# Top-k attention and a hard-swish feed-forward: weighted values queued behind the scores of a later duo, left-over keys first among the scores

## The chip, the cores and the metric

The kernel runs on one core of one Trainium2 chip. The metric is the device time of one execution in microseconds (us). A core has TensorE (PE in the profile; its weight loads are PEld), VectorE (DVE), ScalarE (ACT), GpSimd (POOL) and SyncE (SP), which here issues the DMAs. Each has its own queue of instructions; semaphores hold an instruction until what it needs is there.

## The reference

```python
# attention: q, k, v are (8 batches, 8 heads, 576 positions, 64)
scores = scale * np.matmul(q, k.transpose(0, 1, 3, 2))
kth = np.partition(scores, -32, axis=-1)[..., -32:-31]
scores = np.where(scores >= kth, scores, -1e9)
attn = np.exp(scores - np.max(scores, axis=-1, keepdims=True))
attn = attn / (np.sum(attn, axis=-1, keepdims=True) + 1e-09)
attn_out = np.matmul(attn, v)
# feed-forward: x is (4608 tokens, 512), w_in (512, 2048), w_out (2048, 512)
x = attn_out.transpose(0, 2, 1, 3).reshape(4608, 512)
h = x @ w_in
out = (h * np.clip(h + 3.0, 0.0, 6.0) / 6.0) @ w_out
```

Every row of scores keeps its 32 largest entries. All is float32; the feed-forward weights arrive in a wider type and are converted at the start.

## The kernel before

**Duos.** Two heads make a pair, two pairs a duo. A duo is one tile of 128 queries for two pairs, four heads in all. The 576 positions are 4 x 128 and 64 left over, so besides the usual duos there are *rest* duos, which hold the 64 left-over queries (`self.rest`). There are 80 duos, ten a batch (`per_batch`), numbered `m`. In batches 3 to 6 the rest duos are the third and the eighth of the ten; in the others two rest duos follow each other.

**The steps of a duo.** `scores` (L200) multiplies queries by keys into one PSUM tile of five banks, `big`. In a usual duo each of the four heads has a contraction of 64 and uses half of the array's rows (L227, eight records in the profile, two halves at a time): *row halves*. The 64 left-over keys of a pair's two heads lie side by side in `kr`, with zeros elsewhere, and take one matmul over the full array (L230). A rest duo uses quarters (L215, L217). ScalarE copies the tile to `sc` (L233, L236). `top` (L243) is VectorE's search: four rounds of MAX8 (L250) and MATCH_REPLACE8 (L254) for each pair. Then for each pair `shift` (POOL, L263, L266), `exp` (ACT, L273, L278, L283), `inverse` (DVE, L287), `weights` (POOL, L297 and the copy L306 to 16-bit halves `e16`), `flip` (a transposing DMA from SP, L312, to `t16`), and `join` (a copy to `eT`, L318, by ACT for the first pair and by POOL for the second). `values` (L326) multiplies the weights by v into `pv`: each head writes half of the columns (L338, 40 records): *column halves*. `place` (ACT, L348) copies `pv` to `xT`, the input of the feed-forward.

**Feed-forward.** `feed_forward` (L352) handles a block of 128 tokens: 64 matmuls to `h` (L365) and 16 to `acc` (L385); the profile has two records for each such float32 matmul. It is a generator that gives its matmuls in 16 *pieces*, each of eight matmuls to h or two to acc. ACT makes `g` and `hs` of h (L373, L375), POOL gates them (L379, L380), ACT scales `acc` to `o` (L395) and SP stores it (L397). 36 blocks make 576 pieces.

**Order.** The schedule is written by hand. For each duo the main loop (L562) runs eight *slots*, i = 0 to 7. A slot issues one round of `top`, then what is due, and then pieces. The scores of duo m+1 are issued at slot i = 1 of duo m. The other steps stand in tables of slots, counted from the first slot of their own duo: `usual` (L532), `early` for the first two duos and `soon` for the last two. How many pieces a slot gets follows from `left`, the number that are queued (L595). At i = 3 of the second and third duo of a batch, `load_values` issues eight DMAs for v from SP (L163, L167). They overwrite `vm` and `vr`, so they wait for the last values of the batch before.

**Buffers.** `kq` and the transposed weights, `e16`, `t16`, `eT` and the landing tiles share the pool `kqpool` (L57), 13 buffers of one size. `big` has one buffer in PSUM; `pv`, `h` and `acc` share three.

Of the kernel before, what the change touches and what calls it, by code (L numbers as in the profile page):

```python
# [29 lines left out]
def kernel(  # L30
# [9 lines left out]
    nc = tc.nc  # L40
# [12 lines left out]
    def pool(name, bufs, **kw):  # L53
        return ctx.enter_context(tc.tile_pool(name=name, bufs=bufs, **kw))

    consts = pool("consts", 1)
    kqpool = pool("kq", 13)  # L57
    scpool = pool("sc", 3)
    wkpool = pool("wk", 1)
    mpool = pool("m", 4)  # L60
# [27 lines left out]
    def big():  # L88

        return ps_big.tile([P, 5 * 512], F32, tag="big", name="big")  # L90
# [94 lines left out]
    class Duo:  # L185
# [14 lines left out]
        def scores(self, us=(0, 1)):  # L200

            if us[0] == 0:
                self.sc = scpool.tile([P, 2, 2 * (S + R)], F32, tag="sc", name="sc")
                self.den = mpool.tile([P, 2, 2], F32, tag="den", name="den")
            sc, nu = self.sc[:, us[0] : us[-1] + 1, :], len(us)
            ps = big()
            heads = [slice(0, D), slice(D, P)]
            qs = slice(self.qt * P, min(self.qt * P + P, S))
            banks = ps[:, 0 : 4 * 512].rearrange("p (n s) -> p n s", s=512)
            left = ps[:, 4 * 512 :]  # L210
            if self.rest:
                for i, u in enumerate(us):
                    pr = self.pairs[u]
                    for d in heads:
                        nc.tensor.matmul(banks[d, i, :], pr.qT[d, qs], pr.kT[d, :])  # L215
                    for hh, d in enumerate(heads):
                        nc.tensor.matmul(left[d, i * R : (i + 1) * R], pr.qT[d, qs], pr.kr[d, hh, :])  # L217
                nc.gpsimd.memset(sc[:, :, S : S + R], 0.0)
                nc.scalar.copy(sc[:, :, 0:JP], banks[:, 0:nu, :])
                nc.scalar.copy(  # L220
                    sc[:, :, JP:S], left[:, 0 : nu * R].rearrange("p (u r) -> p u r", r=R)
                )
                return
            for i, u in enumerate(us):
                pr = self.pairs[u]
                for hh, d in enumerate(heads):
                    nc.tensor.matmul(banks[:, 2 * i + hh, :], pr.qT[d, qs], pr.kT[d, :])  # L227
            for i, u in enumerate(us):
                pr = self.pairs[u]
                nc.tensor.matmul(  # L230
                    left[:, i * P : (i + 1) * P], pr.qT[:, qs], pr.kr[:].rearrange("p h r -> p (h r)")
                )
            nc.scalar.copy(  # L233
                sc.rearrange("p u (h s) -> p (u h) s", h=2)[:, :, 0:JP], banks[:, 0 : 2 * nu, :]
            )
            nc.scalar.copy(  # L236
                sc[:, :, JP : JP + P], left[:, 0 : nu * P].rearrange("p (u r) -> p u r", r=P)
            )
# [177 lines left out]
    per_batch = 2 * J + 2  # L416
    ND = len(duos)
# [92 lines left out]
    def pair_at(m, first):  # L510
# [21 lines left out]
    usual = dict(  # L532
        shift0=3, exp0=4, inverse0=9, weights0=10, flip0=12, join0=15,
        shift1=7, exp1=8, inverse1=13, weights1=14, flip1=16, join1=19, values=22, place=23,
    )
    early = dict(
        shift0=3, exp0=3, inverse0=4, weights0=4, flip0=5, join0=8,
        shift1=7, exp1=7, inverse1=8, weights1=8, flip1=9, join1=12, values=12, place=13,
    )
    soon = dict(  # L540
        shift0=3, exp0=3, inverse0=5, weights0=5, flip0=7, join0=10,
        shift1=7, exp1=7, inverse1=9, weights1=9, flip1=11, join1=14, values=16, place=17,
    )
    queued = {}
    for m in range(ND):
        for part, at in (early if m < 2 else soon if m >= ND - 2 else usual).items():
            queued.setdefault(8 * m + at, []).append((m, part))

    def parts(slot, late=None):
# [12 lines left out]
    for m in range(ND + 3):  # L562
        u = duos[m] if m < ND else None
# [70 lines left out]
```

## Time and profile before

| | |
|---|---|
| median of 4 runs | 1582.98 us (1582.19 to 1584.37) |
| the profiled execution: its own time | 1583.64 us |
| the profiled execution: span of its trace | 1581.9 us |
| VectorE busy | 1466.6 us |
| TensorE busy | 1469.5 us |
| ScalarE busy, GpSimd busy | 1092.6 us, 1141.9 us |
| L250, mean of one MAX8 | 744 to 747 ns |
| L385, L365, L338, L227: busy | 524.9, 543.6, 225.7, 135.8 us |
| granted TensorE clock, mean | 0.963 |

The span runs from the first instruction of the trace to its last. The busy time of TensorE is taken from records whose ends are modelled, so that starts are surer than ends. An entry of the timeline gives the start, the time from the first start to the last end of a merged run of instructions, the engine, line and operation, the tiles (out<-in), and in brackets the idle time of the engine just before it with what ended it.

### The profile page before, as it was taken

The page shows a single profiled execution, that of the slowest core. Times are in us where ns is not written, and L with a number is a line of the kernel's source. Part 1 is how long each engine was busy: PE and PEld are TensorE (multiplying, and loading weights), DVE is VectorE, ACT ScalarE, POOL GpSimd, SP SyncE. Part 2 cuts the span into 40 slices and gives each one's busy share as a digit, 9 for nine tenths or more (in the row PEclk, how much of TensorE's full clock was granted, in tenths as well). Part 3 has the DMA queues.
Part 4 walks back from the last instruction along what each step waited for, and adds up shares of the span by engine and source line. Part 5 has one row for each costly group of instructions (what it writes and reads, how often), then busy time and mean ns, then how long its engine had stood idle before and what let it go on. Part 6 is the DMA issues. An engine that isn't in the chain of part 4 may idle for free.

```text
span 1581.9 us, 28785 instructions
## 1 busy us (share of the span) xinstructions
PE 1469.5 (93%) x10272; PEld 1031.1 (65%) x10272; DVE 1466.6 (93%) x3105; ACT 1092.6 (69%) x1865; POOL 1141.9 (72%) x1264
## 2 busy tenths in 40 slices
PE   5256899799999999999999999999999999999899
PEld 2152666467766776766676776777767776767665
DVE  6999999999999999999999999999999999899800
ACT  6675777677776777677776777778767777777521
POOL 4868687677867787777687777877687777867741
PEclk9577799999999999999999999999999999999999
DMA  8652544444444444455344444445353543533410
GB/s 236 163 177 45 112 83 88 86 91 97 76 99 82 97 83 89 88 97 105 65 101 73 97 88 83 92 93 112 57 110 76 97 88 83 97 63 68 82 23 14
DMA packets 450319, 144.49 MB, mean 91 GB/s; under 512 B 433280, under 2 KB 441472, under 8 KB 450176
## 3 DMA queue, kind: packets, MB, share of 16 engines
q1 hardware_dynamic: 450176, 142.65, 44.2%
q8 instruction: 81, 1.33, 0.4%
q14 instruction: 62, 0.51, 0.1%
HBM read 45.09 MB, written 9.44 MB: 34 GB/s over the span
## 4 chain that ended last, share of the span: by engine, by line
PE 54%; DVE 34%; POOL 4%; issue 3%; ACT 3%; DMA 1%; SPq 1%; POOLq 0%; ACTq 0%; DVEq 0%
PE acc L385 20%; PE h L365 20%; DVE m L250 17%; DVE wk L254 14%; PE pv L338 6%; PE big L227 4%; PE big L230 1%; PE big L177 1%; DVE y L118 1%; PE big L215 1%; POOL eT L318 1%; POOL e L306 1%; DMA t<-e 1%; DVE a L117 1%; POOL sc L297 1%
## 5 line engine op out<-in xcount | busy, mean ns | idle before, releaser
L250 DVE MAX8 m<-wk 128x8 f32<-128x576 f32 x864 | 613.6, 747 | 2.2
L385 PE MATMUL acc<-w_out,g 128*128 128x512 f32 x1152 | 524.9, 604 | 15.3 <-POOL g L380 15.3
L365 PE MATMUL h<-xT,w_in 128*128 128x128 f32 x4096 | 484.1, 278 | 3.0 <-ACT xT L348 3.0
L365 PEld LDWEIGHTS h<-xT,w_in 128*128 128x128 f32 x4096 | 471.6, 194 | 17.3 <-issue 11.9
L254 DVE MATCH_REPLACE8 wk<-m,wk 128x576 f32<-128x576 f32 x576 | 424.0, 743 | 0.0
L385 PEld LDWEIGHTS acc<-w_out,g 128*128 128x128 f32 x1152 | 213.1, 193 | 251.6 <-issue 229.3
L297 POOL TENSOR_SCALAR sc<-sc,den 128x576 f32<-128x576 f32 x288 | 213.3, 751 | 192.0 <-DVE den L287 185.1
L306 POOL COPY e<-sc 128x2304 uint16<-128x2304 uint16 (+1 forms) x192 | 320.0, 1676 | 10.1
L278 ACT ACTIVATE sc<-sc,shift 128x576 f32<-128x576 f32 x288 | 220.4, 771 | 28.4 <-POOL shift L266 25.6
L338 PE MATMUL pv<-eT,vm 128*64 128x128 f32 (+1 forms) x2560 | 164.4, 273 | 67.4 <-ACT eT L318 45.2
L318 ACT COPY eT<-t 128x2304 uint16<-128x2304 uint16 (+1 forms) x82 | 216.1, 2635 | 9.3 <-DMA t<-e 9.3
L273 ACT ACTIVATE sc<-sc,m 128x576 f32<-128x576 f32 x288 | 210.4, 780 | 12.1 <-DVE m L250 11.8
L254 DVE MATCH_REPLACE8 wk<-m,sc 128x576 f32<-128x576 f32 x288 | 212.0, 743 | 0.0
L318 POOL COPY eT<-t 128x2304 uint16<-128x2304 uint16 (+1 forms) x78 | 203.8, 2613 | 9.7 <-DMA t<-e 9.6
L250 DVE MAX8 m<-sc 128x8 f32<-128x576 f32 x288 | 203.5, 744 | 4.2 <-ACT sc L236 4.2
L338 PEld LDWEIGHTS pv<-eT,vm 128*64 128x64 f32 x2560 | 135.1, 141 | 104.5 <-ACT eT L318 46.7
L373 ACT ACTIVATE g<-h,three 128x512 f32<-128x512 f32 x144 | 98.3, 683 | 143.5 <-PE h L365 132.5
L380 POOL TENSOR_TENSOR g<-g,hs 128x512 f32<-128x512 f32 x144 | 184.7, 1282 | 12.1
L379 POOL TENSOR_SCALAR g<-g 128x512 f32<-128x512 f32 x144 | 89.0, 618 | 109.9 <-ACT g L373 101.2
L233 ACT COPY sc<-big 128x2048 f32<-128x2048 f32 (+1 forms) x65 | 119.5, 1838 | 38.7 <-PE big L230 38.1
L227 PE MATMUL big<-kq 64*128 64x512 f32 x512 | 135.8, 651 | 8.6 <-ACT kr L183 5.0
L395 ACT ACTIVATE o<-acc 128x512 f32<-128x512 f32 x36 | 21.4, 593 | 112.8 <-PE acc L385 112.8
(47 smaller groups left out, 1117.0 us busy)
## 6 DMA issues: line engine op xcount, KB each, us to landing
landed<-in_k_dram SPq DMA_DIRECT2D x64, 128.0 KB, 2.9
landed<-in_q_dram SPq DMA_DIRECT2D x64, 128.0 KB, 2.9
st<-in_moe_w_in_dram SPq DMA_DIRECT2D x16, 512.0 KB, 5.0
vm<-in_v_dram SPq DMA_DIRECT2D x64, 128.0 KB, 2.3
st<-in_moe_w_out_dram SPq DMA_DIRECT2D x16, 512.0 KB, 5.5
out_dram<-o SPq DMA_DIRECT2D x32, 256.0 KB, 2.4
t<-e SPq DMA_TRANSPOSE x160, 4.6
landed<-in_k_dram SPq DMA_DIRECT2D x32, 32.0 KB, 2.6
```

What stands on the lines that cost most here:

```text
L227: nc.tensor.matmul(banks[:, 2 * i + hh, :], pr.qT[d, qs], pr.kT[d, :])
L250: nc.vector.max(self.m[u][:, t, 8 * r : 8 * r + 8], self.cur[t])
L254: nc.vector.match_replace(wk, self.m[u][:, t, 8 * r : 8 * r + 8], self.cur[t], LOWEST)
L273: nc.scalar.activation(row, row, AF.Prelu, bias=m[:, t, TOP_K - 1 : TOP_K], scale=-1.0, alpha=FLAT)
L278: nc.scalar.activation(row, row, AF.Exp, bias=self.less[u][:, t : t + 1], scale=-scale / FLAT, accum_out=self.den[:, u, t : t + 1],)
L297: nc.gpsimd.tensor_scalar(row, row, self.den[:, u, t : t + 1], 1.0, ALU.mult, ALU.mult)
L306: nc.gpsimd.tensor_copy(halves[:, :, to : to + c1 - c0], words)
L318: copy(eT[:, 0 : self.nb, :] .rearrange("p c q -> p (c q)") .bitcast(U16) .rearrange("p (x h) -> p h x", h=2), self.t16[u][:, 0 : 2 * self ...
L338: nc.tensor.matmul(pv[hh * D : (hh + 1) * D, u * w : (u + 1) * w], pr.vm[:, hh, c, :] if c < J else pr.vr[:, hh, :], rhs, start=(c == 0), ...
L365: nc.tensor.matmul(h[:, (f - f0) * P : (f - f0 + 1) * P], w_in[:, i, f * P : (f + 1) * P], xT[:, i, :], start=(i == 0), stop=(i == NHP - 1),)
L380: nc.gpsimd.tensor_tensor(g[:], g[:], hs[:], ALU.mult)
L385: nc.tensor.matmul(acc[:], gs[f // nf][:, f % nf * P : (f % nf + 1) * P], w_out[:, f, :], start=(f == 0), stop=(f == NFC - 1),)
```

## The change

Three things change.

1. In `scores` of a usual duo the matmuls of the left-over keys (full array) are issued ahead of the row halves instead of after them. The scores of a rest duo stay as they are.
2. A fourth table, `behind`, moves `values` from slot 22 to slot 25 and `place` from slot 23 to slot 26. It holds for duos 10 to 75. Slot 25 of duo m is slot i = 1 of duo m+3, in which the scores of duo m+4 are issued. The values of duo m thus follow these scores directly in TensorE's queue, and a pass in row halves is followed by one in column halves. Blocks of the feed-forward are queued when their `xT` is placed, so they are queued three slots later too.
3. `kqpool` has 14 buffers instead of 13.

```diff
-    kqpool = pool("kq", 13)
+    kqpool = pool("kq", 14)
...
             for i, u in enumerate(us):
                 pr = self.pairs[u]
+                nc.tensor.matmul(
+                    left[:, i * P : (i + 1) * P], pr.qT[:, qs], pr.kr[:].rearrange("p h r -> p (h r)")
+                )
+            for i, u in enumerate(us):
+                pr = self.pairs[u]
                 for hh, d in enumerate(heads):
                     nc.tensor.matmul(banks[:, 2 * i + hh, :], pr.qT[d, qs], pr.kT[d, :])
-            for i, u in enumerate(us):
-                pr = self.pairs[u]
-                nc.tensor.matmul(
-                    left[:, i * P : (i + 1) * P], pr.qT[:, qs], pr.kr[:].rearrange("p h r -> p (h r)")
-                )
...
+    behind = dict(usual, values=25, place=26)
...
-        for part, at in (early if m < 2 else soon if m >= ND - 2 else usual).items():
+        for part, at in (early if m < 2 else soon if m >= ND - 2 else behind if per_batch <= m < ND - 4 else usual).items():
```

In the changed kernel the left-overs are on L226 and the row halves on L232; the lines around them, such as L233 and L338, keep their numbers up to the tables.

More of the change, by code (lines that the diff above doesn't have):

```diff
@@ L225, in scores @@
                 pr = self.pairs[u]
-                for hh, d in enumerate(heads):
-                    nc.tensor.matmul(banks[:, 2 * i + hh, :], pr.qT[d, qs], pr.kT[d, :])
-            for i, u in enumerate(us):
-                pr = self.pairs[u]
                 nc.tensor.matmul(
@@ L232, in scores @@
                 )
+            for i, u in enumerate(us):
+                pr = self.pairs[u]
+                for hh, d in enumerate(heads):
+                    nc.tensor.matmul(banks[:, 2 * i + hh, :], pr.qT[d, qs], pr.kT[d, :])
             nc.scalar.copy(
```

## The prediction

> **What bounds the kernel now.** I read the page first, for who is busy when.
>
> ```profile
> span 1581.9 us, 28785 instructions
> PE 1469.5 (93%) x10272; PEld 1031.1 (65%) x10272; DVE 1466.6 (93%) x3105; ACT 1092.6 (69%) x1865; POOL 1141.9 (72%) x1264
> DVE  6999999999999999999999999999999999899800
> ```
>
> VectorE (the top-32 search) is full from the second slice until about 1497 us and then stops; the last two slices are feed-forward work on TensorE alone. So the end is (a) VectorE's work, (b) the idle time inside it, (c) the tail after it. Next the busy time by stretch:
>
> ```profile
> 200.00:1480.00 1280.00, 1263.95 (x9072) 887.75 (x9072) 1266.49 (x2717) 929.26 (x1589) 958.94 (x1066) 0.99 0.45 87
> ```
>
> The columns are PE, PEld, DVE, ACT, POOL. From 200 to 1480 us VectorE lacks only 13.5 us. The change adds and removes nothing on VectorE, so nothing it does to TensorE before 1480 us is worth more than this. The timeline of VectorE shows the idle places of more than a quarter of a microsecond in this stretch, all of them:
>
> ```profile
> 586.79 0.17 DVE L287 RECIPROCAL den<-den 128x2 f32<-128x2 f32 x1 [1.03 <-ACT den L283]
> 1007.77 1.42 DVE L250 MAX8 m<-sc 128x8 f32<-128x576 f32 x2 [1.51 <-ACT sc L236]
> 1183.94 0.17 DVE L287 RECIPROCAL den<-den 128x2 f32<-128x2 f32 x1 [0.81 <-ACT den L283]
> 1275.59 1.42 DVE L250 MAX8 m<-sc 128x8 f32<-128x576 f32 x2 [0.34 <-ACT sc L236]
> 1376.69 0.16 DVE L287 RECIPROCAL den<-den 128x1 f32<-128x1 f32 x1 [3.38 <-ACT den L283]
> 1379.85 1.42 DVE L250 MAX8 m<-sc 128x8 f32<-128x576 f32 x2 [0.69 <-ACT sc L236]
> ```
>
> They sum to 7.76 us, and each lies in or just after a rest duo, which VectorE passes in 11.2 us instead of 19.4 (distance of the first MAX8 of successive duos). TensorE is behind there. I set the start of each scores group (L227 or L215) against the start of the duo that VectorE is searching: from duo 20 on the distance L is mostly 3 to 10 us, about 6 in the mean, and 8.1 us at 1003 us. The copy to sc ends 4.8 us after the scores begin, so L of 8.1 leaves nothing of a rest duo's 11.2. The den waits are the same lateness through ScalarE: at 579.59 it waited 4.03 us for h (L365), with the exponentials behind it. At 1376 the chain goes through SP:
>
> ```profile
> 1361.14 0.35 SPq L397 DMA_DIRECT2D out_dram<-o  x1
> 1361.58 0.38 SPq L163 DMA_DIRECT2D vm<-in_v_dram  x1
> ...
> 1366.21 8.15 SPq L312 DMA_TRANSPOSE t<-e  x3
> ```
>
> An output store waits for a late ScalarE, eight loads of v follow it in 4.6 us, and only then the transposes go out that join, and ScalarE behind it, wait for.
>
> **Mode switches, and the skill.** The timeline of TensorE around one group of each kind (start, time from first start to last end):
>
> ```profile
> 904.32 1.88 PE L385 MATMUL acc<-w_out,g 128*128 128x512 f32 x4
> 906.13 1.09 PE L338 MATMUL pv<-eT,vm 128*64 128x128 f32 x16
> ...
> 908.46 3.70 PE L385 MATMUL acc<-w_out,g 128*128 128x512 f32 x8
> 912.09 1.99 PE L227 MATMUL big<-kq 64*128 64x512 f32 x8
> 914.01 0.71 PE L230 MATMUL big<-kr,kq 128*128 128x128 f32 x4
> 914.56 3.60 PE L385 MATMUL acc<-w_out,g 128*128 128x512 f32 x8
> ```
>
> In a plain run acc has one start per 0.43 us (the last 32 take 13.75). Eight are 3.44, but 908.46 to 912.09 is 3.63: 0.19 more. Four row pairs are 1.72, but 912.09 to 914.01 is 1.92: 0.20 more. From L230 to acc, without a change of shape, 914.56 + 3.44 meets the next group at 918.0. A switch between full, row-half and column-half mode thus costs about 0.19 us. The Trainium skill agrees in kind: "TensorEngine Tiling (Array Packing)", Key Properties, says "Mode switching requires drain"; it gives no price. "TensorE: Matmul & The Clock Gate", Part 1, says that the array's clock drops when TensorE idles; here the granted clock is 0.91 from 1480 to 1520 us, where TensorE idles 3.02 and 2.49 us, and 32 h matmuls then take 5.32 instead of 3.57. The same page, Architectural detail, has ScalarE and VectorE as strict FIFOs; the ScalarE wait at 579.59 with everything behind it agrees.
>
> **The change, part by part.**
> 1. Left-overs first in every scores group: two switches before (full to row, row to full), two after. The copy waits for the end of the group, whose work is the same 2.5 us. Nothing. At the start, L227 already waits for the kr copies (1.53 us at 9.71 us), so L226 waits no longer.
> 2. Values behind scores, for duos 10 to 75: 66 groups. Before, scores and values cost four switches a duo; after, three. Row to column appears nowhere in the trace of before: between 0 and two ordinary switches (0.38), taken as one, 0.19. TensorE saves 66 x 0.19 = 12.5 us (0 to 25), off the critical path except as lag.
> 3. Place in the queue. The issue orders of both kernels show that ahead of every later scores group TensorE has one values group less (2.33 us and two switches of its own, 2.5 in all) and two or three of the 576 feed-forward pieces less (a piece is (4608 x 0.1116 + 1152 x 0.43)/576 = 1.75 us, so 3.5 to 5.3), because their blocks are queued three slots later. L falls by 6 us or until TensorE runs out of ready work: I expect about 3 in place of 6. ScalarE now waits once a duo for TensorE: its copy of place (L348) comes two slots after the scores copy, and the values end 2.3 us after the scores, while the two copies take 2.1. With L at 3 the scores waits (1.51, 0.34) and ScalarE's waits for h and pv behind 1.03 and 0.81 go: 3.69 us.
> 4. What the later values hold. Loads of v must follow the last values that read the old v: five slots earlier before, two slots now, and behind them on SP stand the transposes, behind those ScalarE's join, then an exponential and VectorE's reciprocal. At a rest duo: values end L + 4.9, the eight loads by L + 8.3, the transpose lands 4.7 later, join 2.8, exponentials 1.9: L + 17.7 against the reciprocal at 11.2 + 12.1 = 23.3. Free up to L = 5.6. At duo 72, where a second rest duo follows, the reciprocal is due at 18.2 and the chain ends at L + 17.2: at L = 3 some 2.0 us of the 4.07 remain. Gain there 2.1.
> 5. One more kq buffer covers eT being held three slots longer. No instruction, and no wait on kq stands in the idle times of VectorE. Nothing.
> 6. Tail. After the last scores TensorE has 57 pieces instead of 55. Its last waits before the end:
>
> ```profile
> 1492.19 1.09 PE L338 MATMUL pv<-eT,vm 128*64 128x128 f32 x16 [3.02 <-POOL eT L318]
> 1493.54 5.32 PE L365 MATMUL h<-xT,w_in 128*128 128x128 f32 x32
> 1502.59 1.15 PE L338 MATMUL pv<-eT,vm 128*64 128x128 f32 x16 [2.49 <-POOL eT L318]
> 1504.10 15.38 PE L385 MATMUL acc<-w_out,g 128*128 128x512 f32 x32
> ```
>
> Pieces ahead of these waits are free, those behind are paid. Behind the second stand, in the new order, 32 more h: +3.57. But on POOL one gate (0.61 + 1.27, with its gaps 1.97) leaves the place ahead of that eT; the weights there wait for VectorE until 1492.5, so eT ends at about 1501.0, 1.6 earlier. Net +2.0 if the clock dips as before, near 0 if it doesn't: taken +1.0.
>
> Sum: -3.7 - 2.1 + 1.0 = -4.8 us. The profiled execution took 1583.64 (span 1581.9), 0.66 above the median of 1582.98; from the median it gives **1578.2**.
>
> **The rivals.** A measurement of this kernel tells about 0.2% from no change, 3.2 us: faster is below 1579.8, slower above 1586.1.
> - As forecast: own range 1574.5 to 1579.8, chance 0.58. The best case is all 7.8 us back and no tail: 1575.2.
> - The gain is hidden: TensorE is 98.7% busy in the bulk, so lag returns within each batch, half of the 7.8 us stay, and the two pieces are paid in full (+3.6): 1582.98 - 3.9 + 3.6 = 1582.7. Chance 0.25. For it: L swings by 5 us within a batch. Against: 0.19 us a duo is saved on top. That row to column drains twice, so that nothing is saved, lands between this and the forecast.
> - Slower, by the loads of v: if L stays above 5.6 at the rest duos, SP's queue stands still at every batch. At L = 7 the four boundaries at duos 32, 42, 52, 62 cost 1.4 each, duo 72 costs 7 + 17.2 - 18.2 - 4.1 = 1.9 more than now, the tail 1.0: 1582.98 + 8.5 = 1591.5. Chance 0.17. For it: before, L was 9 to 10.6 at duos 49 to 52. Against: part 3.
>
> The range reaches from the best case to short of the third case's price: 1574.3 to 1587.5.
>
> **What would show it.** Right: fewer and shorter marks in VectorE's timeline than the 7.76 us above, L near 3, scores followed by column halves with about 0.19 us between, 0.2 us a duo less in TensorE; the end of VectorE near 1491. Wrong: a load of v on SP that waits for pv with transposes behind it and a den wait after each rest duo; or the time from VectorE's last MAX8 to the end longer than now by over 2 us.

## The result and the profile after

| | before | changed |
|---|---|---|
| median of all runs | 1583.48 us (52 runs) | 1581.17 us (32 runs) |
| ratio, 95% interval | | 0.9988 (0.9983 to 0.9993) |
| profiled execution: own time, span | 1583.64, 1581.9 us | 1580.30, 1578.5 us |
| VectorE starts the last duo (79) | 1476.9 us | 1471.6 us |
| VectorE's last MAX8 ends; from there to the end | 1496.6; 85.2 us | 1491.3; 87.2 us |
| idle places of VectorE over 0.25 us, 200 us to last MAX8 | six, 7.76 us | three, 2.97 us |
| lag L of TensorE (explained below), mean of duos 21 to 76 | 6.3 us | 2.3 us |

The change makes the kernel faster by 1.9 us (1.1 to 2.7), which lies within the 0.2% that I had called "no change". The sign was right, the forecast of -4.8 was too large. The ratio is formed from all executions, so it differs a little from that of the medians, which gives 2.3 us. By the profiled executions it is -3.4: -5.35 up to the start of the last duo, +1.98 after VectorE's last MAX8. The changed kernel's profiled execution lies 0.87 below its median; its executions run from 1579.8 to 1584.2.

The page of the changed kernel, the same three lines as before:

```profile
span 1578.5 us, 28787 instructions
PE 1456.9 (92%) x10272; PEld 1039.0 (66%) x10272; DVE 1466.7 (93%) x3105; ACT 1095.8 (69%) x1865; POOL 1142.7 (72%) x1264
DVE  6999999999999999999999999999999999999700
```

VectorE has the same work to 0.1 us. TensorE has 12.6 us less, and 66 switches at 0.19 are 12.5; that the two agree to 0.1 is luck, since the kernels below that save no switch lie anywhere from 1461.1 (e7) to 1472.5 us (e8). The switch is better read from single starts, further down. The busy time by stretch (PE, PEld, DVE, ACT, POOL):

```profile
200.00:1480.00 1280.00, 1257.54 (x9081) 897.97 (x9081) 1271.41 (x2729) 937.15 (x1596) 963.18 (x1071) 0.99 0.45 88
```

VectorE lacks 8.6 us of the 1280 instead of 13.5. The timeline of VectorE in the changed kernel has three idle places over a quarter of a microsecond left:

```profile
420.24 0.16 DVE L287 RECIPROCAL den<-den 128x1 f32<-128x1 f32 x1 [0.87 <-ACT den L283]
1371.32 0.16 DVE L287 RECIPROCAL den<-den 128x1 f32<-128x1 f32 x1 [1.41 <-ACT den L283]
1374.47 1.42 DVE L250 MAX8 m<-sc 128x8 f32<-128x576 f32 x2 [0.68 <-ACT sc L236]
```

The 1.03, 1.51, 0.81 and 0.34 of before are gone, the 3.38 is 1.41, and the place at 420 us is new. They account for 4.79 of the 5.35; VectorE's work being equal, the other 0.56 comes from shorter places. The order on TensorE in the changed kernel, start and time from first start to last end:

```profile
906.27 0.61 PE L226 MATMUL big<-kr,kq 128*128 128x128 f32 x4
906.81 1.99 PE L232 MATMUL big<-kq 64*128 64x512 f32 x8
908.73 1.09 PE L338 MATMUL pv<-eT,vm 128*64 128x128 f32 x16
...
911.06 3.70 PE L385 MATMUL acc<-w_out,g 128*128 128x512 f32 x8
```

Row halves start at 906.81 and column halves at 908.73: 1.92, of which four pairs at 0.43 are 1.72. The direct switch costs 0.20, as an ordinary one does. The distance is 1.92 in 50 of the 52 such groups in the main loop; the other two follow a wait of TensorE.

Between duos 21 and 76, L behaves like this in the profiled executions (start of a scores group on TensorE against the start of the duo that VectorE searches; below zero is ahead of it; a column is headed by the duo whose scores start, and VectorE then searches the duo before it; e1 is the first experiment below):

| duo | 21 | 31 | 37 | 39 | 49 | 57 | 59 | 62 | 69 | 72 |
|---|---|---|---|---|---|---|---|---|---|---|
| before | 7.8 | 7.2 | 5.9 | 5.7 | 9.6 | 6.4 | 5.3 | 5.9 | 8.0 | 7.4 |
| changed | 3.4 | 1.9 | -0.3 | 1.7 | 3.9 | 1.0 | 4.5 | 4.7 | 6.6 | 5.3 |
| e1 | 3.7 | 3.8 | 2.5 | 3.8 | 6.9 | 5.3 | 8.9 | 9.7 | 6.9 | 6.1 |

The change leads before by 3.3 to 6.6 us from duo 21 to 57 (5.1 in the mean) and by 0.2 to 3.4 (1.6) from 59 to 76. What happens at 38 and 58 is on TensorE. First its costliest group of matmuls to h in the changed kernel (before: idle 3.0), then the second of the places in its timeline:

```profile
L365 PE MATMUL h<-xT,w_in 128*128 128x128 f32 x4096 | 485.4, 279 | 17.3 <-ACT xT L348 17.3
```

```profile
733.10 3.39 PE L365 MATMUL h<-xT,w_in 128*128 128x128 f32 x28 [2.66 <-ACT xT L348]
```

TensorE has run out of pieces that are ready: the next block waits for an xT whose values stood behind the scores. It idles 9.3 us at 326.67, 2.66 here and 3.39 at 1089.58, and lead that it idles away is gone. Two things come on top. Of the 5.0 us that it idles around duo 38, the first 2.38 are a wait for `kr`, left-over keys that the scores read, and not for pieces. And the matmuls right behind such a wait are slow:

```profile
723.19 0.71 PE L226 MATMUL big<-kr,kq 128*128 128x128 f32 x4 [2.38 <-ACT kr L183]
723.83 3.20 PE L232 MATMUL big<-kq 64*128 64x512 f32 x8
...
1089.58 5.02 PE L365 MATMUL h<-xT,w_in 128*128 128x128 f32 x28 [3.39 <-ACT xT L348]
```

Row halves take 3.20 instead of 1.99. The 28 h matmuls take 5.02, where as many take 3.39 at 733.10, and the granted clock is 0.84 from 1090 to 1100 us. At duo 58 the 3.39 of idling and the 1.6 of slow matmuls make 5.0, about the 4.6 us by which the lead over before shrinks from duo 57 to 59.

### The profile page after: what moved, and what is told of

The parts are those of the page before. It is cut to its first block, busy times and chain, and to the rows that moved or that the text cites. A ratio compares the mean times of both kernels' runs of the same rounds, so it can differ in the third digit from the quotient of the medians.

```text
span 1578.5 us, 28787 instructions
## 1 busy us (share of the span) xinstructions
PE 1456.9 (92%) x10272; PEld 1039.0 (66%) x10272; DVE 1466.7 (93%) x3105; ACT 1095.8 (69%) x1865; POOL 1142.7 (72%) x1264
## 4 chain that ended last, share of the span: by engine, by line
DVE 45%; PE 43%; POOL 4%; issue 3%; ACT 3%; SPq 1%; DMA 1%; POOLq 0%; ACTq 0%; DVEq 0%
DVE m L250 23%; DVE wk L254 19%; PE h L365 17%; PE acc L385 16%; PE pv L338 5%; PE big L232 3%; DVE y L118 1%; PE big L177 1%; POOL e L306 1%; DVE a L117 1%; PE big L215 1%; POOL sc L297 1%; PE big L226 1%; POOL eT L318 1%; DMA t<-e 1%
## 5 line engine op out<-in xcount | busy, mean ns | idle before, releaser
L385 PE MATMUL acc<-w_out,g 128*128 128x512 f32 x1152 | 516.9, 600 | 14.1 <-POOL g L380 14.1
L306 POOL COPY e<-sc 128x2304 uint16<-128x2304 uint16 (+1 forms) x192 | 320.0, 1676 | 10.1
L338 PE MATMUL pv<-eT,vm 128*64 128x128 f32 (+1 forms) x2560 | 164.0, 273 | 58.0 <-ACT eT L318 45.8
L338 PEld LDWEIGHTS pv<-eT,vm 128*64 128x64 f32 x2560 | 135.2, 141 | 109.4 <-ACT eT L318 49.8
L232 PE MATMUL big<-kq 64*128 64x512 f32 x512 | 136.5, 653 | 0.0
L233 ACT COPY sc<-big 128x2048 f32<-128x2048 f32 (+1 forms) x65 | 119.2, 1834 | 24.9 <-PE big L232 24.6
```

Of the source, the lines that this page charges most:

```text
L306: nc.gpsimd.tensor_copy(halves[:, :, to : to + c1 - c0], words)
L338: nc.tensor.matmul(pv[hh * D : (hh + 1) * D, u * w : (u + 1) * w], pr.vm[:, hh, c, :] if c < J else pr.vr[:, hh, :], rhs, start=(c == 0), ...
L385: nc.tensor.matmul(acc[:], gs[f // nf][:, f % nf * P : (f % nf + 1) * P], w_out[:, f, :], start=(f == 0), stop=(f == NFC - 1),)
```

## The experiments

All ratios are to the kernel before, run beside it. The experiments were run in three groups (e1 to e4, e5 to e8, e9 to e11), each on another chip, so kernels are compared by these ratios. "Places" are VectorE's idle places over 0.25 us from 200 us on, L is the mean over duos 21 to 76; these and the last column come from one profiled execution each, which for e1 lies 2.1 us above its median and for e2, e5, e7 and e9 2.4, 3.1, 2.2 and 1.3 below.

| | ratio (95%) | median us | places us | L us | last MAX8 to end us |
|---|---|---|---|---|---|
| changed | 0.9988 (0.9983, 0.9993) | 1581.17 | 2.97 | 2.3 | 87.2 |
| e1 | 1.0024 (1.0015, 1.0033) | 1586.73 | 10.1 | 4.6 | 88.5 |
| e2 | 1.0001 (0.9993, 1.0010) | 1583.77 | 6.0 | 5.8 | 85.2 |
| e3 | 1.0038 (1.0025, 1.0050) | 1589.56 | 14.9 | 6.3 | 83.4 |
| e4 | 1.0038 (1.0024, 1.0051) | 1590.04 | 12.9 | 5.2 | 86.4 |
| e5 | 0.9970 (0.9958, 0.9982) | 1579.14 | 1.1 | 3.0 | 85.6 |
| e6 | 0.9965 (0.9953, 0.9977) | 1576.59 | 0.8 | 2.8 | 85.7 |
| e7 | 0.9978 (0.9971, 0.9985) | 1579.80 | 5.3 | 6.2 | 82.1 |
| e8 | 1.0034 (1.0022, 1.0046) | 1589.50 | 11.2 | 5.9 | 88.6 |
| e9 | 1.0013 (1.0006, 1.0019) | 1585.42 | 5.3 | 3.9 | 88.6 |
| e10 | 0.9987 (0.9981, 0.9994) | 1581.05 | 2.4 | 3.5 | 88.1 |
| e11 | 1.0020 (1.0012, 1.0027) | 1586.15 | 12.3 | 5.9 | 83.7 |

**e1: the values behind the scores, but without the saved switch.** Against the changed kernel, the left-over keys go last again, so row halves are followed by a full-array group before the column halves: four switches a duo, as before.

```diff
             for i, u in enumerate(us):
                 pr = self.pairs[u]
+                for hh, d in enumerate(heads):
+                    nc.tensor.matmul(banks[:, 2 * i + hh, :], pr.qT[d, qs], pr.kT[d, :])
+            for i, u in enumerate(us):
+                pr = self.pairs[u]
                 nc.tensor.matmul(
                     left[:, i * P : (i + 1) * P], pr.qT[:, qs], pr.kr[:].rearrange("p h r -> p (h r)")
                 )
-            for i, u in enumerate(us):
-                pr = self.pairs[u]
-                for hh, d in enumerate(heads):
-                    nc.tensor.matmul(banks[:, 2 * i + hh, :], pr.qT[d, qs], pr.kT[d, :])
```

> Only the values moved behind the scores (with 14 kq buffers); the left-overs stay last among the scores, so scores and values of a duo cost TensorE four mode switches as before, not three: about 0.19 us a duo, 12.5 us in all, more than in the changed kernel. Theory A (what counts is how much stands ahead of the scores in TensorE's queue, not the switches): scores begin on average 2.3 to 3.3 us after the start of the duo that VectorE searches (6.3 before, 2.3 in the changed kernel), VectorE's idle places over 0.25 us between 200 us and its last MAX8 sum to 2 to 4 us (7.8 before, 3.0 changed), time 0.9982 to 0.9994 of before. Theory B (the saved switches brought the gain): lag of 4 us or more, idle places of 6 us or more, time 1.000 to 1.002 of before, because the longer tail stays.

Measured: slower than before, by 3.8 us at the ratio of 1.0024 (3.1 by the medians), and 0.0036 (5.7 us) above the changed kernel. In the table of L, e1 and the changed kernel start out together; from duo 23 to 37 their distance grows from 0.70 to 2.76 us, which over the 11 usual duos among these 14 is 0.19 each: the price of one switch. By duo 62 e1 stands at 9.7. Then VectorE pays, as its timeline in e1 shows:

```profile
1186.06 0.17 DVE L287 RECIPROCAL den<-den 128x2 f32<-128x2 f32 x1 [3.65 <-ACT den L283]
```

So the new place in the queue gives a lead once, and TensorE idles much of it away (17.2 us of waits for xT in e1, as in the changed kernel). What holds the lead over the 66 duos is the saved switch. Without it the change loses. The mean of L does not set VectorE's idle time by itself: e1 has less of it than the kernel before (4.6 against 6.3) and more idle time (10.1 against 7.8 us). Whether its peaks after duo 58 or the later place of the values is to blame was not separated. The fourteenth buffer was not run alone; e1 has it, and is slower.

**e2: only the left-overs first.** The first part of the change on the kernel before, with its tables and 13 buffers.

> Only the left-over keys go first among the scores; values stay at slot 22, 13 kq buffers. Theories A and B: two switches around every scores group as before, lag about 6.3 us, idle places 7 to 8.5 us, 0.9995 to 1.0005 of before. A third theory, that the order inside the scores group itself brings something (the copy of the scores starting earlier): lag unchanged, but idle places fall by 1 us or more and the time to 0.999 or below.

Measured: 1.0001. Two switches before, two after; nothing, as the prediction's part 1 has it.

**e3: hold pieces back instead.** The kernel before, with two pieces kept in the queue in the main loop, to give TensorE a shorter queue ahead of the scores without moving the values.

```diff
-            due += ((left > 0) + (left >= 24) / 8 + (left >= 48) / 8) / (2 if u and u.rest else 1)
+            due += ((left > (2 if m < ND else 0)) + (left >= 24) / 8 + (left >= 48) / 8) / (2 if u and u.rest else 1)
```

> The kernel before with one number changed: a slot gets feed-forward pieces only if more than 2 are queued (left > 2 in place of left > 0), so that TensorE has two pieces (3.5 us) less ahead of nearly every later scores group, without values moved and with four switches a duo. One piece more (56 for 55) stands after the last scores. Theory A: lag near 6.3 - 3.5 = 2.8 to 3.3 us, idle places fall from 7.8 to 2.5 to 4.5 us, tail longer by 0 to 1.8 us; together 0.9976 to 0.9990 of before. Theory B: idle places stay above 6 us, time 1.000 to 1.001. If lag falls but the idle places stay, the lag isn't their cause.

Measured: slower by 0.0038, with L unchanged at 6.3. So it does not isolate the lead. The likely reason is that the held pieces were missing where TensorE had nothing else: its waits ahead of L338 rose from 67.4 us to 81.5. The largest idle place of VectorE is again at duo 73:

```profile
1385.52 0.17 DVE L287 RECIPROCAL den<-den 128x1 f32<-128x1 f32 x1 [7.86 <-ACT den L283]
```

**e4: shorten the tail.** The changed kernel with `left >= 20` in place of `left >= 24`: 55 pieces after the last scores, as in the kernel before, not 57.

> The changed kernel with the bound at which a slot gets more pieces lowered from 24 to 20 queued: up to duo 60 the same number of pieces ahead of the scores (to within one), but 55 pieces instead of 57 after the last scores. Theory A (the two pieces are paid in full behind the last wait for eT): the last such wait to the end takes 79 to 80.5 us as before (82.8 in the changed kernel), 1576.5 to 1579 us, 0.9960 to 0.9975 of before. Rival C (the tail is set by the clock's dip or by GpSimd, whatever the pieces): 82 us or more, 0.9983 to 0.9993 as the changed kernel.

Measured: slower by 0.0050 than the changed kernel. The tail itself did get shorter: from the last wait for eT to the end it takes 80.6 us instead of 82.8, though the granted clock fell to 0.83 there. But L rises to 5.2, and the pieces gained behind the last scores cost more ahead of them. SP's queue in e4, and what VectorE makes of it at the same duo:

```profile
1367.43 0.35 SPq L397 DMA_DIRECT2D out_dram<-o  x1
1367.87 0.38 SPq L163 DMA_DIRECT2D vm<-in_v_dram  x1
...
1372.50 7.78 SPq L312 DMA_TRANSPOSE t<-e  x3
```

```profile
1382.64 0.16 DVE L287 RECIPROCAL den<-den 128x1 f32<-128x1 f32 x1 [7.30 <-ACT den L283]
```

An output store waits for ScalarE until 1367.43, the eight loads of v need 4.6 us behind it, and then the transposes go out. Their join on ScalarE waited 5.69 us and started at 1378.0. This is the prediction's part 4, at a larger L.

**e5 and e6: clear SP's queue.** e5 is the changed kernel with the loads of v two slots later. e6 also issues the output stores from ScalarE's queue.

```diff
-            if i == 3 and u and u.pairs[0].b and 1 <= m % per_batch <= 2:
+            if i == 5 and u and u.pairs[0].b and 1 <= m % per_batch <= 2:
...
-                        nc.sync.dma_start(dst, o[p0:p1, :])
+                        nc.scalar.dma_start(dst, o[p0:p1, :])
```

> The changed kernel with the loads of v issued at slot i = 5 in place of i = 3, so that they stand behind the transpose of slot i = 4 in SP's queue. Theory D (lag of TensorE becomes idle time of VectorE through SP's queue: a load of v that waits for pv holds the transposes behind it): the 2.1 us at duos 73 and 74 fall to 0.5 or less, the 0.9 us near 420 us stays (an output store stands there), sum below 1.5 us, time 0.9970 to 0.9982 of before (1.4 to 2.1 us below the changed kernel). Rival (TensorE's lag reaches VectorE without SP): 2 us or more stay, 0.9985 to 0.9993 as the changed kernel.

> As the run before, and the output stores are issued from ScalarE's queue right behind the o that they store, so that SP never waits for acc. Theory D: no idle place over 0.5 us between 200 us and VectorE's last MAX8, sum below 1 us, 0.9965 to 0.9980 of before. Against it: each store costs ScalarE some 0.4 us of issue, 36 of them; if that delays exponentials, idle places of 1 us or more come at other duos and the time is no better than with the loads moved alone.

Measured: 0.9970 and 0.9965. In e5 both places at duos 73 and 74 (1.41 and 0.68) are gone, the one at 420 us is 0.60, and a new one of 0.51 stands at 1474. In e6 the one at 420 is below a quarter microsecond too; 0.51 at 1475 and 0.29 at 1269 are what is left. SP's queue in e6, at the same boundary:

```profile
1350.38 9.04 SPq L312 DMA_TRANSPOSE t<-e  x2
1359.51 0.53 SPq L163 DMA_DIRECT2D vm<-in_v_dram  x1
```

Two transposes now go out from 1350.38 on, ahead of these loads. By e5, which moves nothing else, the loads are the cause of what remained at duos 73 and 74. Whether moving the stores adds to that is not settled: the intervals of e5 and e6 overlap. Of e5's five executions two took 1576.0 and 1576.7 with a mean clock of 0.966 and 0.965, and three 1579.1 to 1580.6 with 0.961 or 0.962. e6 has the lowest ratio of all that was run.

**e7: the same two edits on the kernel before.**

> The kernel before (values at slot 22, left-overs last, 13 buffers) with loads of v at i = 5 and stores from ScalarE. Theory D: the 4.07 us at duos 73 and 74 go to below 1, those where the scores themselves are late (1.51 and 0.34 us) stay, sum 2 to 4.5 us, time 0.9970 to 0.9985 of before; TensorE's lag stays near 6.3. Rival: only less lag helps, so idle places stay above 6 us and the time within 0.9993 to 1.0007.

Measured: 0.9978. The change is worth 0.0012 alone and 0.0013 on top of these edits (0.9978 to 0.9965); the edits are worth 0.0022 and 0.0023. The two gains seem to add up, but the intervals of e6 and e7 overlap, so that the second 0.0013 is not clear of noise. L stays at 6.2 in e7, and with it places such as 1.70 us at 587 and 1.52 at 1275.

**e8: the same two edits on e1.** If lag turns into idle time of VectorE only by way of SP, this mends e1.

> Values behind scores but left-overs last (one switch more a duo than the changed kernel), with loads of v at i = 5 and stores from ScalarE. Without the two it was 1.0024 of before, with 10.1 us of idle places and a mean lag of 4.6 us. Theory D: the lag stays 4 to 5 us, idle places fall below 3 us, time 0.9970 to 0.9990 of before. Rival: lag as such sets the idle places, 7 us or more stay, 1.001 to 1.003.

Measured: 1.0034, no better than e1. That theory (D in the expectations) fell as the only way; the loads of v in e5 remain a case of it. ScalarE's timeline in e8, and then VectorE's:

```profile
901.23 0.69 ACT L373 ACTIVATE g<-h,three 128x512 f32<-128x512 f32 x1 [2.50 <-PE h L365]
...
909.35 0.69 ACT L373 ACTIVATE g<-h,three 128x512 f32<-128x512 f32 x1 [1.50 <-PE h L365]
```

```profile
916.28 0.17 DVE L287 RECIPROCAL den<-den 128x2 f32<-128x2 f32 x1 [2.23 <-ACT den L283]
```

ScalarE stands still for h while TensorE is behind, and the exponentials queued behind it are late with no DMA in between. The Trainium skill, "TensorE: Matmul & The Clock Gate", Architectural detail, calls ScalarE a strict FIFO; 2.50 and 1.50 us of waits ahead of a place of 2.23 agree.

**e9 and e10: place one slot earlier.** `behind = dict(usual, values=25, place=25)`, on the changed kernel and on e6. It gives xT a slot earlier, to spare TensorE the waits for it (theory E in the expectations).

> The changed kernel with place at slot 25, right behind its values, in place of 26: the feed-forward block and its xT come one slot earlier (for most duos one piece more stands ahead of a scores group). Theory E: the lead that TensorE has won is lost where the queue of pieces is nearly empty and h waits for xT (5.0 us of idle TensorE at duo 38, 3.4 at duo 58 in the changed kernel, each with slower matmuls behind it); with place earlier these waits fall to below 2 us each and the lag at duos 59 to 74 is 1.5 us or more below the 4.5 to 7.3 of the changed kernel; the idle places of VectorE then fall from 3.0 to 1.5 us or less, 0.9972 to 0.9985 of before. Rival: ScalarE, waiting for pv a slot earlier, delays the exponentials, or the one piece more (1.75 us) eats it up: lag at duos 59 to 74 unchanged or higher, time as the changed kernel or slower (0.9985 or above).

> As the run before, with loads of v at i = 5 and stores from ScalarE, which alone gave 0.9965. If TensorE's lag no longer reaches VectorE once SP is free (idle places were below 1 us there), place makes no difference: 0.9958 to 0.9972. If ScalarE's earlier wait for pv hurts, 0.9975 or above.

Measured: 1.0013 and 0.9987, both slower than their counterparts (0.9988 and 0.9965). The waits for xT are 15.5 us in e9, TensorE's idle time at duos 38 and 58 stays (5.6 and 3.3 us, against 5.0 and 3.4 in the changed kernel). At duo 38 the wait for xT does fall, from 2.66 to 1.45 us, but the wait for kr rises from 2.38 to 4.11. L rises to 3.9, and the place at duo 73 is 3.55 us. E fell: TensorE still runs dry, and since blocks are queued earlier too, a piece more stands ahead of most scores.

**e11: the shorter tail on e6.** e4's `left >= 20`, with SP's queue cleared.

> The run with the bound 20 (55 pieces after the last scores), which alone took 1.0038 of before with 12.9 us of idle places, now with loads of v at i = 5 and stores from ScalarE. If those 12.9 us came through SP (the store and the loads of v ahead of the transpose at duo 72, 7.3 us), they fall to 1 to 4 us and the time is 0.9955 to 0.9975 of before. If they came through ScalarE directly, 8 us or more stay and the time is 1.001 or above.

Measured: 1.0020, 0.0055 above e6. The 7.30 us of e4 are gone, but seven places of up to 2.50 us are there, with L at 5.8. Pieces put ahead of the scores turn into idle time of VectorE with or without SP.

## Why the forecast was right in direction and too large

The median of 1581.17 us lies in the range that was given over all cases, but outside the forecast's own (1574.5 to 1579.8), and nearer to the 1582.7 of the hidden gain than to 1578.2. The mechanism of parts 1 to 4 is in the main what the traces show. In two terms a right number was partly luck, as parts 4 and 6 tell.

1. **Left-overs first: nothing.** Right (e2).
2. **The switch.** Its price was taken as 0.19 and is 0.20; TensorE saves some 12.5 us. The Trainium skill, "TensorEngine Tiling (Array Packing)", Key Properties, says that a mode switch requires a drain; the trace shows that going straight from row to column halves costs as much as one such switch, not two. What I got wrong is its weight. I wrote that a change without the saving would land between the hidden gain and the forecast. e1 has as many switches as that kernel, and it is slower than before by 3.8 us: the switch is worth 5.7 us of the end.
3. **The place in the queue.** L of "about 3" came out at 2.3. The 3.69 us of idle places at 586, 1007, 1183 and 1275 are all gone. But the lead shrinks where TensorE runs out of ready pieces, at duos 15, 38 and 58, so from duo 59 to 74 it is mostly 4 to 7 again (2.2 to 7.3). The sentence that L falls "until TensorE runs out of ready work" was right; that this happens three times, and what it leaves behind, I had not worked out.
4. **The loads of v.** 2.0 us were to remain at duos 73 and 74; 1.41 + 0.68 = 2.10 did. The chain was right, the number in part luck. The chain ended 17.1 us after the scores of duo 73 began, where 17.2 was forecast. But these scores began 4.4 us after VectorE started duo 72, not 3, and the reciprocal was due 20.1 us after that start, not 18.2 (the profile of before has 20.1 too: 1376.69 less the wait of 3.38, against a start at 1353.22). The two errors nearly cancel. SP's queue of the changed kernel:

```profile
1357.47 0.33 SPq L163 DMA_DIRECT2D vm<-in_v_dram  x1
...
1362.05 2.71 SPq L312 DMA_TRANSPOSE t<-e  x1
```

   The first load waits for the values, the transpose goes out 4.6 us later, the reciprocal starts at 1371.32. e5 takes the place away by moving only these loads.
5. **What was missed: 0.87 us at 420.** There a store of o goes out at 408.46 and a transpose behind it at 408.93; in the kernel before, this transpose went out at 406.31, and in e6, where the stores are off SP, at 406.50. The place is 0.60 in e5, where the store still goes out from SP, and below 0.25 in e6. I had put the stores of o nowhere in the sum.
6. **The tail, the term that was mis-sized.** I took +1.0 between 0 and +2.0; it was +1.98. TensorE's timeline of the changed kernel at its last wait:

```profile
1495.68 1.82 PE L338 MATMUL pv<-eT,vm 128*64 128x128 f32 x16 [4.41 <-POOL eT L318]
...
1497.86 4.51 PE L365 MATMUL h<-xT,w_in 128*128 128x128 f32 x32
1502.21 10.47 PE L385 MATMUL acc<-w_out,g 128*128 128x512 f32 x24
```

   From that wait to the end are 82.8 us instead of 79.3: the two pieces are paid in full, +3.5. The clock dips as before: pv takes 1.82 for 1.09 and the h matmuls 4.51 for 3.57, 1.7 us together. eT is ready 4.4 us after the last MAX8 instead of 5.9. So the sum of +2.0 with a dip of the clock came out, but the reason that I gave for the earlier eT, the gate that leaves GpSimd, is not needed for it. GpSimd's timeline in the changed kernel, where the gate is gone, and in e7, where it is still there:

```profile
1487.27 1.47 POOL L297 TENSOR_SCALAR sc<-sc,den 128x576 f32<-128x576 f32 x2 [2.37 <-DVE den L287]
```

```profile
1489.68 1.48 POOL L297 TENSOR_SCALAR sc<-sc,den 128x576 f32<-128x576 f32 x2 [0.31 <-DVE den L287]
```

   The 2.37 us that GpSimd waits for VectorE exceed the gate's 1.97, and in e7 eT is ready after 4.4 us too. In the kernel before GpSimd was late because the transpose was: its join at 1489.38 waited 1.88 us for it. So a transpose that lands on time is enough for the 1.5 us. Where the clock does not dip, the tail does not come out level, as I had thought that it would: e6 and e7 have a clock of 1.00 there, and 85.7 against 82.1 us, +3.6. The +1.98 also lies at the very line of 2 us that the prediction had named as a sign of being wrong.

By the profiled executions the sum is then -5.35 + 1.98 = -3.4 where I had -5.8 + 1.0 = -4.8. Of the miss of 1.4, 1.0 is the tail and 0.87 the place at 420, with half a microsecond back from short places. The medians put it at -2.3 and the ratio at -1.9, the rest being where in its spread the profiled execution fell.

Of the rivals, the hidden gain (1582.7) had the two pieces right, but 38% of the idle places remain, not half. The slow case by the loads of v did not come, since L at the boundaries at duos 32, 42, 52 and 62 was 3.5, 2.0, 2.6 and 4.7, under the 5.6 from which it was to decide. That figure does not hold itself: the reciprocals are due 16.8 and 26.5 us after the start of duo 32, not 23.3. e4 shows its chain at duo 73 with 7.30 us.

What stays open is why TensorE runs dry just at duos 38 and 58: earlier places (e9, e10) did not mend it, and no other cure was tried, neither for xT nor for the wait for kr at duo 38.

## What to carry to other kernels

An engine that is nearly as full as the bounding one must be judged by how far it runs behind, duo by duo, and not by its busy time: 0.19 us a duo on TensorE, off the critical path in each single duo, decided between 1.9 us faster and 3.8 us slower. Here the lead won by reordering was spent where that engine ran out of ready work, and only less work held it. When a step is moved later, look at what each in-order queue (SP, ScalarE) issues behind its last reader, and price the tail as work that is paid in full unless a wait behind it shows idle time.

## What the runs showed of the hardware

- A switch straight from row halves to column halves costs as much as one between row halves and the full array: 0.20 us here, against 0.19 and 0.20. In rest duos the same holds for quarters: from the start of the last four quarter matmuls to the first in column halves (changed kernel) are 0.21 us, as to the first of the full array (before).
- Matmuls behind a wait of TensorE can be slow although the wait is short: after 2.38 us eight row halves took 3.20 us instead of 1.99 in the changed kernel, and after 3.39 us 28 h matmuls took 5.02, where after a wait of 2.66 us as many took 3.39.
- The clock's dip in the tail comes and goes between kernels that idle alike: after a wait of 3.02 us 32 h matmuls took 5.32 us in the kernel before (granted clock 0.91 from 1480 to 1500 us), after one of 3.03 us they took 3.84 in e6 (1.00). TensorE's timeline in e6:

```profile
1493.40 1.09 PE L338 MATMUL pv<-eT,vm 128*64 128x128 f32 x16 [3.03 <-POOL eT L318]
1494.65 3.84 PE L365 MATMUL h<-xT,w_in 128*128 128x128 f32 x32
```

  In the tail of the changed kernel it is worth 1.7 us. Its coming and going may be part of the spread between executions of one kernel; that was not tried.
- Eight small loads with nothing to wait for after the first hold SP's queue for 4.6 us, some 0.57 each.
